# Attention, ELU layer and gated layer on one core: which slots are handed out first at a stage border, where weight conversion runs, and the order of VectorE's work beside the gated products

## The chip, the cores and the metric

The kernel runs on one core of a Trainium2 chip. The metric is the device time of one execution in microseconds (us); the profile's times are counted from the first instruction of the profiled execution. Engines are TensorE (PE), VectorE (DVE), ScalarE (ACT), GpSimd (POOL) and SyncE (SP). SP and POOL issue the transfers here, each from a queue of its own in program order.

## The reference

Chunked attention (chunks of 64) on q, k, v of shape 8 x 8 x 576 x 64, then two dense layers on the 4608 x 512 result:

```python
attn = softmax(q_c @ k_c.T / 8)              # per chunk of 64
x = (attn @ v_c).transpose(0, 2, 1, 3).reshape(4608, 512)
h = x @ w_in                                 # 512 -> 2048
x = where(h > 0, h, exp(min(h, 0)) - 1) @ w_out      # 2048 -> 512
out = (sigmoid(x @ w_gate) * (x @ w_val)) @ w_out2   # 512 -> 1536 -> 512
```

## The kernel before, in words

Every engine executes its instructions in the order in which the code emits them (a manual schedule); engines meet only through semaphores. There are four stages.

**Stage 1** (to about 511 us in the profile) walks nine blocks of 512 tokens. A block has eight slots, one for each 256 columns of the first layer. A slot `d` has the attention of one pair of tiles on PE and then 24 matmuls of the first layer (L380, `layer_in`) into one of three PSUM banks. The ELU of the slot before is taken by ACT (L394, L397) and VectorE (L402) into a tile of the pool `e`, which has four tiles, and stored by SP as `gd<-elu` (L405). The attention is done one block early, so in the last block only the layer and the ELU remain; that block is emitted by `stage_2` through `one`.

**Weight conversion.** The float64 weights of the later layers are converted on the chip in 26 pairs of tiles (`convert_pairs`). A pair has 12 steps in the list `todo`; `bg(n)` emits the next n of them between other work. A step is a few operations of ACT and VectorE; a pair loads two raw tiles (`craw`) and stores seven sums (`wd_glu<-ch` for the gate and value weights). A store is issued by POOL and waits for VectorE. Pairs 0 to 16 are spread over stage 1's slots, pairs 17 to 19 are begun in its last block, pairs 20 to 25 in stage 3.

**Weight fetches.** The 28 tiles of the pool `w` are shared by the 16 tiles of the first layer, the conversion's tiles and the fetched weights of the later stages. `hold(at, room, ahead)` emits, on POOL's queue, the fetches (L324) of the next `ahead` weight tiles that the products will use, never holding more than `room`; `room(7)` leaves 7 of the 28 tiles to the conversion. What does not fit is dropped and fetched again when its turn comes.

**Stage 2** (511 to 876 us) is the second layer. A round j (six of them, each for 768 tokens) has seven products i, each in four parts p; a part is 12 matmuls (L692) with one weight tile and one tile `gc`. The tile for part p of product i+1 is made beside part p of product i: a cast on ACT (L92) and a subtraction on VectorE (L98), of data that SP loads as `b<-gd` and VectorE has added up (L676). All these tiles are 6 KB slots per partition ("sixes"): ten on the right side and four on the left, where the first layer's inputs and the ELU tiles of stage 1 have lain. `get` takes the next slot from the list `idle`, `free` puts one back at its end. A left slot can be written only when the stores of the ELU tiles under it have read them.

**Stage 3** (876 to 1413 us) is gate and value: 36 units of seven products (banks x, w, y, z, x, y, z), each 12 matmuls (L828). Products 4 to 6 add onto banks of products 0 to 3, so product 5 (bank y) cannot start before VectorE has read bank y after product 2. VectorE adds the banks up (L101) and forms gate times value (L880, L882, `finish`). Six units share their inputs; in the sixth ("last") the next six's inputs are split (cast on ACT, L98 on VectorE) and in the fourth ("third" in the code, from the end) their sums are formed. **Stage 4** is the output layer (L960).

Names of the part that the change touches:

```python
PAIRS_1, PAIRS_2 = 17, HF + 2 * QU           # 17 and 20
need = list(soon)[:min(ahead, room)]         # in hold
p = idle.pop(0)                              # in get
```

Of the kernel before, what the change touches and what calls it, by code (L numbers as in the profile page):

```python
# [27 lines left out]
F1 = DFF1 // 128  # L28
# [6 lines left out]

LEAD = 11
EARLY = 2
PRE_STEPS = (0, 0, 1, 1, 1, 1, 1, 1, 1, 1, 2, 1)
W_AT = (1, 4)
IN_STEPS = 3  # L40
# [17 lines left out]
def kernel(  # L58
# [41 lines left out]
    def add(out, a, b):  # L100
        nc.vector.tensor_tensor(out=out, in0=a, in1=b, op=ALU.add)  # L101
# [3 lines left out]
    def bg(n):  # L105
        for _ in range(min(n, len(todo))):
            todo.pop(0)()
# [222 lines left out]
    def open_sixes(side, n):  # L330
        six[side] = ctx.enter_context(tc.tile_pool(name=f"six_{side}", bufs=n, side=side, reuse_waits="tile"))
        idle.extend([side] * n)

    def shaped(t, shape):
# [3 lines left out]
        names = " ".join("abc"[:len(shape)])  # L338
        return t[:, 0:n].rearrange(f"p ({names}) -> p {names}", **dict(zip("abc", shape)))

    def get(key, shape, dtype=F32):
        p = idle.pop(0)
        t = six[p].tile([128, 1536], dtype, tag="six", name=key)
        v = shaped(t, shape)
        owner[id(v)] = p, v
        return v
# [7 lines left out]
    def stage_1():  # L354
# [60 lines left out]
        with (  # L415
# [194 lines left out]
            convert_pairs(range(PAIRS_1), nc.gpsimd)  # L610
            end = (NB - 1) * HF
            for d in range(HF, end):
                slot(d, -(-len(todo) // (end - d)))
            assert not todo
        pb.close()
        return one
# [1 line left out]
    def room(*busy):  # L618
        return NW - sum(busy)
# [30 lines left out]
    def stage_2(one):  # L650
# [131 lines left out]

        open_sixes("right", 10)
        end = NB * HF
        convert_pairs(range(PAIRS_1, PAIRS_2), nc.gpsimd)
        for n in range(HF):
            one(end - HF + n, True)
            if n in (0, 2, 4):
                load_b(0, ("b11", "b12", "b22")[n // 2])
            if 2 <= n <= 5:  # L790
                split_b(0, 0, n - 2)
            if n >= 6:
                sub_b(0, "b11", "b12", "b11", n - 6)
            bg(3)
            hold(0, room(F1 - 2 * n - 2, 7), n + 2)
        for j in range(NJ):
            for i in range(7):
                for p in range(QM):
                    product(j, i, p)
                    if j == i == p == 0:  # L800
                        one(end, False)
                        pa.close()
                        open_sixes("left", 4)
                        three_p = ctx.enter_context(
                            tc.tile_pool(name="three", bufs=3, side="right", reuse_waits="tile")
                        )
                    beside(j, i, p)
                    if j == NJ - 1:
                        for f in first_x.get((i, p), ()):
                            f()  # L810
                    if i in (2, 3, 5) and p > 0:
                        bg(2)
                    hold((7 * j + i) * QM + p + 1, room(7 if todo else 0), 10)
                after(j, i)
        assert not todo and not raw and not gc

# [2 lines left out]
    def unit(n):  # L819
        j, q = seq[n]  # L820
        last, third = n % QU == QU - 1, n % QU == QU - 3
        for i, c in enumerate(PRODUCTS):
            ps = bank[c][:, :, 0:NL]
            w = held["glu", q, i]
            for b in range(2):
                for k in range(2):
                    for p, (zw, zx) in enumerate(PASSES):
                        nc.tensor.matmul(  # L828
                            out=ps[:, b],
                            lhsT=w[:, b, zw, 128 * k:128 * k + 128],  # L830
                            rhs=xc[j, i][:, zx, k],
                            start=(i < 4 and k == 0 and p == 0),
                            stop=(k == 1 and p == 2),
                            skip_group_check=True,
                        )
            if last:
                free(xc.pop((j, i)))
            yield
            hold(MID + 7 * n + i + 1, room(7 if todo else 0), 14 if n < len(seq) - 3 else 22)
            if i == 0:  # L840
                s, t = get("s", (2, 2, NL)), get("t", (2, 2, NL))
                u, v, c12 = s[:, 0], s[:, 1], t[:, 0]

                def sigmoid(x, of=None):
                    nc.scalar.activation(out=x, in_=x if of is None else of, func=ACTF.Sigmoid)  # L845

                nc.scalar.copy(out=u, in_=ps)  # L847
                while pending:
                    pending.pop(0)()
            elif i == 1:  # L850
                add(u, ps, u)
            elif i == 2:
                add(v, ps, u)
            elif i == 3:
                add(v, ps, v)
                sigmoid(v[:, 0])
            elif i == 4:
                sigmoid(t[:, 1, 0], ps[:, 0])
                nc.vector.tensor_tensor(out=t[:, 1, 0], in0=ps[:, 1], in1=t[:, 1, 0], op=ALU.mult)
            elif i == 5:  # L860
                add(c12, ps, u)
                sigmoid(c12[:, 0])
            else:
                add(u, ps, u)
                sigmoid(u[:, 0])
            bg(1)
            if j + 1 < NJ:
                if n % QU == 1 and i >= 5:
                    load_x(j + 1, i - 5)
                if third and 1 <= i <= 3:  # L870
                    sum_x(j + 1, i)
                if last:
                    if i == 6:
                        sum_x(j + 1, 4)
                    split_x(j + 1, i)
                    if i == 6:
                        done_x(j + 1)

        def finish():
            nc.vector.tensor_tensor(out=s[:, :, 0], in0=s[:, :, 1], in1=s[:, :, 0], op=ALU.mult)  # L880
            nc.sync.dma_start(out=gvd[j][:, 0:2, q], in_=s[:, :, 0])
            nc.vector.tensor_tensor(out=c12[:, 0], in0=c12[:, 1], in1=c12[:, 0], op=ALU.mult)  # L882
            nc.sync.dma_start(out=gvd[j][:, 2:4, q], in_=t[:, :, 0])
            free(s)
            free(t)
        pending.append(finish)

    def stages_3_4():
# [82 lines left out]
        def after(g, i):  # L971
# [28 lines left out]
                del ut[g], ot[g]  # L1000

        N = len(seq)
        before = {
            (N - 2, 1): lambda: load_g(0, "c12"),
            (N - 2, 2): lambda: load_g(0, "c22"),
            (N - 1, 1): lambda: load_g(0, "c11"),
            (N - 1, 2): lambda: sum_1(0),
            (N - 1, 3): lambda: load_g(0, "c21"),
            (N - 1, 5): lambda: (split_g(0, 0, "c11", keep=True), sum_2(0)),
        }  # L1010
        for n in range(N):
            if n == 2:
                hold(MID + 7 * n, room(7), 14)
                convert_pairs(range(PAIRS_2, len(tiles_of)), nc.sync)
            for i, _ in enumerate(unit(n)):
                before.get((n, i), lambda: None)()
        for g in range(G):
            for i in range(7):
                prepare(g, i)
# [68 lines left out]
```

## Time and profile before

| | |
|---|---|
| median of 3 runs | 1690.31 us (1690.2 to 1693.1) |
| the profiled execution's own time | 1689.72 us |
| its span, first to last instruction | 1688.0 us |
| PE busy | 1632.2 us, 97% of the span |
| VectorE, ACT, POOL busy | 1214.1, 744.6, 224.0 us |
| mean granted TensorE clock | 0.991 |
| transferred | 367.83 MB, 218 GB/s over the span |

The profiled execution takes 1.72 us more than its span and is 0.59 us under the median. PE is busy nearly throughout, so a saving can only come from the stretches in which it stands still or runs on a lower clock; those must be looked for stretch by stretch.

### The profile page before, as it was taken

What the parts mean: (1) busy time and instruction counts of PE and PEld (TensorE: products, weight loads), DVE (VectorE), ACT (ScalarE), POOL (GpSimd) and SP (SyncE); (2) the same over time, 40 slices, a digit from 0 to 9 for tenths busy, and PEclk for the clock granted to TensorE, in tenths of its full rate; (3) what the DMA queues carried; (4) which work ended last, traced back from release to release, by engine and by line L of the source; (5) the groups of instructions that cost most, each with busy time, mean ns of one, the idle gap of its engine ahead of it and who ended that gap; (6) DMA issues with size and microseconds to landing.
All of it is one profiled execution on the core that took longest, in us unless ns stands there. A gap on an engine that the chain in (4) does not pass through costs nothing.

```text
span 1688.0 us, 28556 instructions
## 1 busy us (share of the span) xinstructions
PE 1632.2 (97%) x11484; PEld 1527.7 (91%) x11484; DVE 1214.1 (72%) x1660; ACT 744.6 (44%) x1184; POOL 224.0 (13%) x368
## 2 busy tenths in 40 slices
PE   5899999999997999999999999999999999999998
PEld 4667777777786999999999999999999999999998
DVE  6878888887765877777776877656565646777776
ACT  4766767666663444444442433322131313333333
POOL 3322111211022100000121121201010120000000
PEclk9999999999998999999999999999999999999999
DMA  6558888888599943352897689757263598464541
GB/s 222 193 189 293 296 295 280 284 276 264 195 366 391 330 143 128 113 178 96 250 285 249 208 301 316 255 187 236 83 212 113 181 302 245 123 167 119 164 137 51
DMA packets 225972, 367.83 MB, mean 218 GB/s; under 512 B 13744, under 2 KB 133552, under 8 KB 224816
## 3 DMA queue, kind: packets, MB, share of 16 engines
q1 hardware_dynamic: 169344, 203.46, 37.2%
q0 software_dynamic: 56496, 162.55, 29.2%
q8 instruction: 90, 1.47, 0.4%
q14 instruction: 42, 0.34, 0.1%
HBM read 233.31 MB, written 132.64 MB: 217 GB/s over the span
## 4 chain that ended last, share of the span: by engine, by line
PE 77%; DVE 8%; DMA 6%; ACT 4%; issue 3%; POOL 1%; SPq 1%; ACTq 0%; DVEq 0%; POOLq 0%
PE bank_x L828 7%; PE bank_y L828 7%; PE bank_z L828 7%; PE bank_y L692 6%; PE bank_z L692 6%; PE bank_y L380 6%; PE bank_x L692 5%; PE bank_w L380 5%; PE bank_z L380 5%; PE bank_y L960 5%; PE bank_z L960 5%; PE bank_x L960 4%; PE bank_w L828 3%; PE bank_w L692 3%; DMA w<-wd_glu 2%
## 5 line engine op out<-in xcount | busy, mean ns | idle before, releaser
L98 DVE TENSOR_TENSOR gc<-b,gc 128x768 fp32r<-128x768 f32 x144 | 134.1, 954 | 61.8 <-ACT gc L92 60.5
L92 ACT CAST gc<-b 128x768 fp32r<-128x768 f32 x144 | 117.2, 834 | 129.3 <-PE bank_y L692 46.1
L828 PE MATMUL bank_y<-xc,w 128*128 128x384 f32 x864 | 163.7, 338 | 8.1 <-DVE s L101 7.5
L828 PE MATMUL bank_x<-xc,w 128*128 128x384 f32 x864 | 161.7, 336 | 0.5 <-ACT s L847 0.5
L828 PE MATMUL bank_z<-xc,w 128*128 128x384 f32 x864 | 161.9, 336 | 0.0
L828 PEld LDWEIGHTS bank_y<-xc,w 128*128 128x128 f32 x864 | 152.1, 189 | 9.7 <-DVE s L101 8.7
L828 PEld LDWEIGHTS bank_x<-xc,w 128*128 128x128 f32 x864 | 150.7, 188 | 1.1 <-ACT s L847 0.8
L828 PEld LDWEIGHTS bank_z<-xc,w 128*128 128x128 f32 x864 | 151.4, 188 | 0.0
L845 ACT ACTIVATE s<-s 128x384 f32<-128x384 f32 x72 | 37.8, 526 | 255.1 <-DVE s L101 255.1
L380 PE MATMUL bank_y<-xs,w 128*128 128x512 f32 x576 | 141.5, 401 | 4.8 <-ACT w L92 3.1
L324 POOL DMA_DIRECT2D w<-wd_glu x126 | 67.3, 537 | 583.9 <-PE bank_x L692 257.1
L380 PE MATMUL bank_w<-xs,w 128*128 128x512 f32 x576 | 139.8, 398 | 0.9 <-POOL w L98 0.9
L380 PE MATMUL bank_z<-xs,w 128*128 128x512 f32 x576 | 139.0, 397 | 0.0
L380 PEld LDWEIGHTS bank_y<-xs,w 128*128 128x128 f32 x576 | 108.8, 192 | 28.4 <-ACT w L92 3.5
L380 PEld LDWEIGHTS bank_w<-xs,w 128*128 128x128 f32 x576 | 107.1, 189 | 23.4 <-POOL w L98 1.2
L380 PEld LDWEIGHTS bank_z<-xs,w 128*128 128x128 f32 x576 | 107.8, 190 | 22.4
L101 DVE TENSOR_TENSOR s<-bank_z,s 128x768 f32<-128x768 f32 x72 | 68.8, 956 | 47.7 <-PE bank_z L828 47.1
L692 PE MATMUL bank_y<-gc,w 128*128 128x384 f32 x576 | 102.2, 336 | 0.0
L692 PE MATMUL bank_x<-gc,w 128*128 128x384 f32 x576 | 102.0, 336 | 0.0
L692 PE MATMUL bank_z<-gc,w 128*128 128x384 f32 x576 | 102.0, 336 | 0.0
L692 PEld LDWEIGHTS bank_y<-gc,w 128*128 128x128 f32 x576 | 100.4, 188 | 0.0
L692 PEld LDWEIGHTS bank_x<-gc,w 128*128 128x128 f32 x576 | 100.2, 188 | 0.1
(144 smaller groups left out, 2961.2 us busy)
## 6 DMA issues: line engine op xcount, KB each, us to landing
w<-wd_glu POOLq DMA_DIRECT2D x126, 512.0 KB, 6.7
gd<-elu SPq DMA_DIRECT2D x72, 512.0 KB, 3.6
c<-gv SPq DMA_DIRECT2D x72, 384.0 KB, 4.9
wd_glu<-ch POOLq DMA_DIRECT2D x36, 512.0 KB, 5.3
b<-gd SPq DMA_DIRECT2D x24, 768.0 KB, 7.1
w<-wd_mid POOLq DMA_DIRECT2D x32, 512.0 KB, 13.4
raw<-in_qkv SPq DMA_DIRECT2D x61, 256.0 KB, 3.9
gv<-s SPq DMA_DIRECT2D x36, 384.0 KB, 5.0
```

The lines of the kernel that those rows point to most:

```text
L92: nc.scalar.copy(out=out, in_=raw)
L98: lo_eng.tensor_sub(out=lo, in0=raw, in1=hi)
L101: nc.vector.tensor_tensor(out=out, in0=a, in1=b, op=ALU.add)
L324: nc.gpsimd.dma_start(out=t, in_=wd[m][q][:, (RIGHT if m == "out2" else LEFT)[i]])
L380: nc.tensor.matmul(out=h_bank(d)[:, n], lhsT=w[:, zw, kk * 128:(kk + 1) * 128], rhs=xs[j, kk][:, zx], start=(kk == 0 and p == 0), stop=(kk ...
L692: nc.tensor.matmul(out=bank[PRODUCTS[i]][:, u, 0:NL], lhsT=w[:, k, zw, 128 * u:128 * u + 128], rhs=t[:, zx, k], start=(i < 4 and p == 0 an ...
L828: nc.tensor.matmul(out=ps[:, b], lhsT=w[:, b, zw, 128 * k:128 * k + 128], rhs=xc[j, i][:, zx, k], start=(i < 4 and k == 0 and p == 0), sto ...
L845: nc.scalar.activation(out=x, in_=x if of is None else of, func=ACTF.Sigmoid)
L960: nc.tensor.matmul(out=po[c][:, m], lhsT=t[:, zx, q % 3, 128 * m:128 * m + 128], rhs=w[:, q % 2, zw], start=(i < 4 and q == 0 and p == 0 a ...
```

## The change

Five things are done.

1. **Slots.** While the first product of the first round of stage 2 runs (`right_first` is filled), `get` takes a right slot if one is idle, and a left one otherwise. Afterwards the order is that of the list again.
2. **Conversion in stage 1.** Pairs 0 to 16 are finished four slots earlier; in those last four slots of block 7 one weight tile more is held ahead in each. In block 8, where 2 to 9 tiles were held ahead and at most 7 + 2n, 5 to 12 are held ahead.
3. **Pairs 17 to 19** are not begun in block 8 any more, but at the start of round 1 of stage 2, and their steps run in rounds 1 and 2; 8 tiles instead of 7 are left to them.
4. **Gate and value.** The conversion's steps pause in each last and third unit, and 9 tiles instead of 7 are left to it. `finish` of a unit moves behind the addition of the next unit's product 1, `sum_x(.., 4)` moves from product 6 to 5, and the loads and sums for stage 4 (`beside`) are emitted behind a product's evacuation and earlier by one to two units for the loads.
5. Line numbers move by up to 9.

```diff
+SLACK = 4
 ...
+    right_first = []
     def get(key, shape, dtype=F32):
-        p = idle.pop(0)
+        p = idle.pop(idle.index("right") if right_first and "right" in idle else 0)
...
             for d in range(HF, end):
-                slot(d, -(-len(todo) // (end - d)))
+                slot(d, -(-len(todo) // max(end - SLACK - d, 1)))
+                if d >= end - SLACK:
+                    hold(0, room(F1), d - end + SLACK + 1)
...
-        convert_pairs(range(PAIRS_1, PAIRS_2), nc.gpsimd)
         for n in range(HF):
             one(end - HF + n, True)
...
-            bg(3)
-            hold(0, room(F1 - 2 * n - 2, 7), n + 2)
+            hold(0, room(F1 - 2 * n - 2), SLACK + 1 + n)
...
                     if j == i == p == 0:
                         one(end, False)
                         pa.close()
+                        right_first.append(True)
                         open_sixes("left", 4)
...
-                    if i in (2, 3, 5) and p > 0:
+                    if (j, i, p) == (1, 0, 0):
+                        hold(7 * QM, room(8), 10)
+                        convert_pairs(range(PAIRS_1, PAIRS_2), nc.gpsimd)
+                    if i in (2, 3, 5) and p > 0 and j > 0:
                         bg(2)
-                    hold((7 * j + i) * QM + p + 1, room(7 if todo else 0), 10)
+                    hold((7 * j + i) * QM + p + 1, room(8 if todo else 0), 10)
+                right_first.clear()
                 after(j, i)
...
-            yield
-            hold(MID + 7 * n + i + 1, room(7 if todo else 0), 14 if n < len(seq) - 3 else 22)
+            hold(MID + 7 * n + i + 1, room(9 if todo else 0), 14 if n < len(seq) - 3 else 22)
...
                 nc.scalar.copy(out=u, in_=ps)
+            elif i == 1:
+                add(u, ps, u)
                 while pending:
                     pending.pop(0)()
-            elif i == 1:
-                add(u, ps, u)
...
-            bg(1)
+            if not last and not third:
+                bg(1)
...
                 if last:
-                    if i == 6:
+                    if i == 5:
                         sum_x(j + 1, 4)
                     split_x(j + 1, i)
...
+            yield
...
-        before = {
-            (N - 2, 1): lambda: load_g(0, "c12"),
-            (N - 2, 2): lambda: load_g(0, "c22"),
-            (N - 1, 1): lambda: load_g(0, "c11"),
+        beside = {
+            (N - 4, 0): lambda: load_g(0, "c12"),
+            (N - 3, 0): lambda: load_g(0, "c22"),
+            (N - 2, 0): lambda: load_g(0, "c11"),
             (N - 1, 2): lambda: sum_1(0),
-            (N - 1, 3): lambda: load_g(0, "c21"),
-            (N - 1, 5): lambda: (split_g(0, 0, "c11", keep=True), sum_2(0)),
+            (N - 1, 3): lambda: (load_g(0, "c21"), sum_2(0)),
+            (N - 1, 5): lambda: split_g(0, 0, "c11", keep=True),
```

PE's instructions and their order are the same. What moves on the other engines is shown at three places.

ACT at the border from stage 1 to stage 2, before: the last ELU, the four casts for product 1 of round 0 (`gc`), the copy of product 0. What stands in brackets are the semaphores that the instruction waits for; `DMAHW0` to `DMAHW7` are those that SP's transfers use in turn, and the last ELU store of stage 1 has `DMAHW1`, the fourth last `DMAHW6`.

```order
L394 ACTIVATE elu<-bank_z 128x1024 [waits DMAHW1_49,PE_49]
L397 ACTIVATE elu<-elu 128x1024 [waits Activation_49]
L92 CAST gc<-t_5745 128x768 [waits DVE_49]
L92 CAST gc<-t_5745 128x768 [waits DMAHW6_49,DMAHW1_49]
L92 CAST gc<-t_5783 128x768 [waits DVE_49]
L92 CAST gc<-t_5783 128x768 [waits PE_49]
```

The same place in the changed kernel:

```order
L397 ACTIVATE elu<-bank_z 128x1024 [waits DMAHW1_49,DVE_49,PE_49]
L400 ACTIVATE elu<-elu 128x1024 [waits Activation_49]
L93 CAST gc<-t_5675 128x768 [waits DVE_49]
L93 CAST gc<-t_5675 128x768 [waits PE_49]
L93 CAST gc<-t_5707 128x768 [waits DMAHW6_49,DMAHW1_49,DVE_49]
L93 CAST gc<-t_5707 128x768 [waits PE_49]
```

The wait for the ELU stores has moved from the second cast (part 1) to the third (part 2); the second waits for PE alone.

POOL's queue from the last pair of stage 1 on, before (`craw` are raw tiles to convert, `wd_glu<-ch` converted sums to store, `w<-wd_mid` weight fetches for stage 2):

```order
L277 DMA wd_glu_86<-ch 128x2x512 x2
L196 DMA craw<-in_w_val 128x1024 x2
L324 DMA w<-wd_mid_78 128x1024
L324 DMA w<-wd_mid_79 128x1024
L196 DMA craw<-in_w_gate 128x1024 x2
L324 DMA w<-wd_mid_80 128x1024
L277 DMA wd_glu_86<-ch 128x2x512
L324 DMA w<-wd_mid_81 128x1024
L277 DMA wd_glu_86<-ch 128x512
L277 DMA wd_glu_86<-ch 128x2x512 x2
```

In the changed kernel all 28 fetches of round 0 follow that pair, and the first raw tile comes behind them:

```order
L278 DMA wd_glu_86<-ch 128x2x512 x2
L325 DMA w<-wd_mid_78 128x1024
L325 DMA w<-wd_mid_79 128x1024
L325 DMA w<-wd_mid_80 128x1024
L325 DMA w<-wd_mid_81 128x1024
...
L197 DMA craw<-in_w_val 128x1024 x2
L325 DMA w<-wd_mid_78 128x1024
L197 DMA craw<-in_w_gate 128x1024 x2
L325 DMA w<-wd_mid_79 128x1024
```

Between a fetch and the next there is no store that waits for VectorE any more until round 1. Over the program POOL has 57 fetches of `wd_mid` instead of 32 and 139 of `wd_glu` instead of 126.

VectorE in the first last unit (unit 5) of gate and value, before (L101 adds a bank up, L98 splits the next inputs, L276, L217 and L221 are conversion):

```order
L98 TENSOR_TENSOR xc<-x,xc 128x768
L101 TENSOR_TENSOR s<-bank_w,s 128x768
L276 TENSOR_TENSOR ch<-cs,ch 128x2x256
L98 TENSOR_TENSOR xc<-x,xc 128x768
L101 TENSOR_TENSOR s<-bank_y,s 128x768
L276 TENSOR_TENSOR ch<-cs,ch 128x2x256
L98 TENSOR_TENSOR xc<-x,xc 128x768
L101 TENSOR_TENSOR s<-bank_z,s 128x768
L217 TENSOR_SCALAR ct<-ct 128x1024
```

The same unit in the changed kernel (L102 is the addition, L99 the split, L889 and L891 are `finish`):

```order
L99 TENSOR_TENSOR xc<-x,xc 128x768
L102 TENSOR_TENSOR s<-bank_w,s 128x768
L889 TENSOR_TENSOR s<-s 128x2x384
L891 TENSOR_TENSOR t<-t 128x384
L99 TENSOR_TENSOR xc<-x,xc 128x768
L102 TENSOR_TENSOR s<-bank_y,s 128x768
L99 TENSOR_TENSOR xc<-x,xc 128x768
L102 TENSOR_TENSOR s<-bank_z,s 128x768
L99 TENSOR_TENSOR xc<-x,xc 128x768
```

One conversion operation per product is gone from this unit, and `finish`, which stood ahead of the addition of bank w, now stands behind it.

## Rows read from the trace of the kernel before

**Rows 1.** The page: span, and busy time of TensorE.
```profile
span 1688.0 us, 28556 instructions
PE 1632.2 (97%) x11484; PEld 1527.7 (91%) x11484; DVE 1214.1 (72%) x1660; ACT 744.6 (44%) x1184; POOL 224.0 (13%) x368
```
**Rows 2.** Windows: length, busy us of each engine, granted clock, DMA share, GB/s.
```profile
0.00:50.00 50.00, 30.50 (x436) 21.98 (x440) 31.53 (x63) 25.18 (x52) 18.29 (x35) 0.97 0.57 196
50.00:130.00 80.00, 70.12 (x611) 54.55 (x601) 65.80 (x108) 53.36 (x89) 20.82 (x20) 0.96 0.63 210
...
500.00:540.00 40.00, 27.76 (x130) 25.03 (x129) 19.87 (x23) 13.29 (x17) 11.19 (x20) 0.83 1.12 388
540.00:880.00 340.00, 340.00 (x1958) 340.00 (x1957) 262.38 (x259) 146.59 (x187) 22.31 (x41) 1.00 0.60 196
```
**Rows 3.** Timeline of TensorE at the border: start, duration, instructions, idle before.
```profile
511.02 8.48 PE L692 MATMUL bank_x<-gc,w 128*128 128x384 f32 x48
...
533.85 9.14 PE L692 MATMUL bank_w<-gc,w 128*128 128x384 f32 x36 [12.24 <-ACT gc L92]
542.84 8.53 PE L692 MATMUL bank_y<-gc,w 128*128 128x384 f32 x48
551.20 8.48 PE L692 MATMUL bank_z<-gc,w 128*128 128x384 f32 x48
```
**Rows 4.** Timeline of ACT at the border.
```profile
532.97 0.83 ACT L92 CAST gc<-t 128x768 fp32r<-128x768 f32 x1 [15.84 <-DMA gd<-elu]
```
**Rows 5.** The chain that ended last, its piece at the border: start, length.
```profile
514.63 18.32 DMA gd<-elu
```
**Rows 6.** Transfers from 460 to 545 us: totals, and issues with median us to landing.
```profile
DMA packets 16034, 31.60 MB, mean 372 GB/s; under 512 B 975, under 2 KB 7110, under 8 KB 16031
...
w<-wd_mid POOLq DMA_DIRECT2D x23, 512.0 KB, 13.5
gd<-elu SPq DMA_DIRECT2D x11, 512.0 KB, 9.4
```
**Rows 7.** The ELU stores' line over the whole run: us from issue to landing.
```profile
DMA to landing us min/median/max: 3.0/3.6/19.1
```
**Rows 8.** Timeline of TensorE in gate and value and into stage 4.
```profile
949.54 2.24 PE L828 MATMUL bank_x<-xc,w 128*128 128x384 f32 x12
...
1054.04 3.75 PE L828 MATMUL bank_y<-xc,w 128*128 128x384 f32 x12 [2.04 <-DVE s L101]
...
1076.70 2.24 PE L828 MATMUL bank_x<-xc,w 128*128 128x384 f32 x12
...
1397.46 2.24 PE L828 MATMUL bank_x<-xc,w 128*128 128x384 f32 x12
...
1423.59 4.44 PE L960 MATMUL bank_y<-w,gc 128*128 128x256 f32 x36
1427.87 2.40 PE L960 MATMUL bank_z<-w,gc 128*128 128x256 f32 x19
```
**Rows 9.** Window of round 2 of stage 2; columns as in rows 2.
```profile
628.00:686.50 58.50, 58.50 (x339) 58.50 (x338) 43.43 (x41) 24.06 (x30) 0.00 (x0) 1.00 0.40 136
```
**Rows 10.** VectorE by line and form: count, busy us, mean ns, idle before.
```profile
L98 DVE TENSOR_TENSOR xc<-x,xc 128x768 fp32r<-128x768 f32 x42 | 40.1, 955 | 19.6 <-ACT xc L92 19.5
L859 DVE TENSOR_TENSOR t<-bank_x,t 128x384 f32<-128x384 f32 x36 | 20.0, 556 | 39.9 <-ACT t L845 39.9
L221 DVE TENSOR_SCALAR ct<-ct 128x1024 uint32<-128x1024 uint32 x26 | 17.9, 690 | 0.5
L276 DVE TENSOR_TENSOR ch<-ct,ch 128x256 fp32r<-128x256 f32 x26 | 10.9, 418 | 0.0
```
**Rows 11.** Timelines of VectorE and TensorE in unit 18, behind a last unit without conversion.
```profile
1157.16 0.96 DVE L101 TENSOR_TENSOR s<-bank_y,s 128x768 f32<-128x768 f32 x1
...
1160.02 2.24 PE L828 MATMUL bank_y<-xc,w 128*128 128x384 f32 x12
```
**Rows 12.** Timeline of POOL in block 8.
```profile
489.55 0.72 POOL L277 DMA_DIRECT2D wd_glu<-ch  x1 [18.24 <-DVE ch L276]
```

More of the change, by code (lines that the diff above doesn't have):

```diff
@@ L1012, in stages_3_4 @@
             if n == 2:
-                hold(MID + 7 * n, room(7), 14)
+                hold(MID + 7 * n, room(9), 14)
                 convert_pairs(range(PAIRS_2, len(tiles_of)), nc.sync)
             for i, _ in enumerate(unit(n)):
-                before.get((n, i), lambda: None)()
+                beside.get((n, i), lambda: None)()
         for g in range(G):
```

## The prediction

> **What bounds the kernel now.** The page's totals come first: TensorE is busy 1632.2 of 1688.0 us [rows 1], so 55.8 us of standing still is all that any edit of the other engines can win, apart from matmuls on the lower clock. The windows say where these lie [rows 2]. The first 130 us lose 19.50 and 9.88 us; the change moves nothing there (the first step it moves stands in slot 44 of 72). From 500 to 540 us 12.24 us are missing, and the granted clock is 0.83. From 540 to 880 us, all of stage 2 behind the border, nothing is missing: 340.00 of 340.00. What is left lies in gate and value and at its end.
>
> *The border.* In TensorE's timeline [rows 3] product 0 of round 0 starts at 511.02 and product 2 at 542.84. A product of 48 matmuls takes 8.36 us (542.84 to 551.20), so two should have taken 16.72; they took 31.82. So 15.10 us are lost: 12.24 in one wait in front of part 1 of product 1, and 2.7 because the 36 matmuls behind it took 8.99 us where 36/48 of 8.36 are 6.27. The wait is for a cast on ACT, and that waited 15.84 us for the store of an ELU tile [rows 4]. The chain shows the store: issued at 514.63, it lands 18.32 us later [rows 5]. Such a store lands after 3.6 us in the median of the run, 3.0 at the least [rows 7]; around the border the median of eleven is 9.4, with 31.60 MB moved in 85 us, at 372 GB/s [rows 6]. So two things make the wait: a slot that needs the last store is wanted early, and the store is slow because the transfers are saturated.
>
> *Gate and value.* Unit 13 starts at 1076.70 and unit 35 at 1397.46: 22 units in 320.76 us, 14.58 each, undisturbed. Units 5 to 12 (949.54 to 1076.70) took 127.16 where eight take 116.64: 10.52 us lost, in waits like that at 1054.04 for VectorE's addition, and in slower matmuls behind them. From 1397.46 to the third product of stage 4 (1423.59) it took 26.13, where a unit and two products of 4.28 (1423.59 to 1427.87) are 23.14: 2.99 lost [rows 8]. In reach are thus 15.10 + 10.52 + 2.99 = 28.6 us.
>
> **The change, part by part.**
>
> *Slots at the border.* The part that needs the last store becomes part 2 of product 1 instead of part 1; the other casts wait for TensorE or VectorE only, as the order shows. The store itself is issued when it was, about 514.63, since the ELU in front of it hangs on TensorE alone. Part 2 is due when product 0 and two parts of 2.09 us (8.36 / 4) are through: 511.02 + 8.36 + 4.18 = 523.56. The cast takes 0.83 [rows 4], and VectorE's subtraction 0.95, of which the first two passes need nothing; so the store must land by about 521.7 to cost nothing, which leaves it 7.1 us. With the shift alone and the store as slow as before, the wait shrinks by 2.09 us only, so the rest must come from the next part.
>
> *Conversion out of block 8, fetches brought forward.* For three pairs, six raw tiles of 0.5 MB and 21 sums of 0.25 MB leave the stretch: 3.1 + 5.5 = 8.7 MB, less the part that lay outside. The weight fetches stay the same 28 x 0.5 MB, but POOL, with no store that waits for VectorE between them, may issue them as tiles of the first layer come free, two in a slot of 5.5 us, and be nearly through when the last store is issued. From 467 to 514 us I count about 16 fetches (8 MB, less the last ones), nine ELU stores (4.7 MB) and three loads of `b` (4.7 MB): 17 MB in 47 us, 360 GB/s against 372 granted [rows 6]. Most of the three loads lies before 505 us, so the last two slots ask for less than is granted, and the queue should be short at 514.63. I take a landing between 3.6 us [rows 7] and 7.1, hence no wait at all and no slower matmuls behind it: 15.1 us gained. The bounds: 9.4 us, the median under saturation [rows 6], leaves 2.3 us of waiting; 18.32 leaves 11.2 and the slow matmuls.
>
> Against the second half of this stands the Trainium skill, page "DMA: Bandwidth & Descriptors", section "Issuing engines are not separate DMA queues": transfers of all issuing engines run on the same 16 DMA engines and interleave. By that, fetches issued earlier on POOL's queue take their bandwidth from the ELU stores and loads on SP's, and if POOL pours out all fetches it may, the store could stay at the saturated latency; the sum would then be 2.3 us worse.
>
> *Conversion in stage 1, four slots earlier.* 204 steps over 52 slots instead of 56 are 4 in a slot almost throughout, where before 4 fell to 3 after 36 slots. TensorE loses nothing while 4 steps run in each slot, so I cost it at nothing; the cover is VectorE's free time there.
>
> *Pairs 17 to 19 in rounds 1 and 2.* A pair has nine VectorE operations of some 0.69 us and five of 0.42 [rows 10]: 8.3 us, so 1.5 pairs in a round are 12.4. Round 2 of before has VectorE busy 43.43 of 58.5 us [rows 9]; with that it is 55.9, still under 58.5. A slot is free again when its product's part is done and due three parts (6.3 us) later; cast and subtraction take 1.8 of that, so a lag of up to some 4.5 us is hidden. Products 2, 3 and 5 carry 6 steps each, about 4.1 us on top of four subtractions and an addition (4.8): 8.9 against 8.36, a lag of 0.5 us each. Nothing lost; if the cover goes, the next product waits by what exceeds 4.5. The 25 additional fetches (13 MB) and the 8.7 MB of the pairs in two rounds of 58.5 us are 185 GB/s on top of 136 [rows 9], together 321, below what was granted at the border. Cost nothing; bound 0 to 33 us (second rival).
>
> *Gate and value.* A unit has five additions of 0.96, `finish` of 0.96 + 0.56, and a product of 0.56 (the 0.56 by the half-wide row): 6.9 us. A last unit adds seven splits and one sum of 0.955: 14.5 of 14.58, no room. Before, seven conversion steps lay on top (7/12 of 8.3, 4.8 us) in units 5 and 11: 19.3 us of work in 14.58. That is the lag which ends in the waits. In units 17, 23 and 29 of before there are no steps, and no wait: in unit 18 the addition of bank y ends at 1158.12, and the product that overwrites it starts at 1160.02, 1.9 us later [rows 11]. The changed units 5 and 11 are like these. Two steps of the next unit (1.4 us) now stand ahead of that addition in units 6, 12 and 18, but the sum moved to product 5 spares ACT's wait for it, about 0.9; margin 1.4. So I take 10.0 of the 10.52, keeping 0.5 for these three places. The 13 more fetches of `wd_glu` (6.7 MB over 16 units, 29 GB/s) I cost at nothing.
>
> *Into stage 4.* `sum_2` runs two products earlier and the additions no longer stand behind it. What stays is the first split: behind the addition of c12 (0.96), a sigmoid (0.5) and the cast (0.83) it comes 2.3 us after product 5, when product 6 takes 2.08; with the low part about 0.7 us. So 2.3 of 2.99 gained; bounds 0 and 2.99.
>
> **Sum.** 15.1 + 10.0 + 2.3 = 27.4 us, from the profiled execution's own time: 1689.72 - 27.4 = 1662.3. That execution lies 0.6 us under the median of the runs, so I say 1663.
>
> **The rivals.**
> 1. *The store stays late.* For it: all fetches may now press into the same 45 us, and the store still stands in the way of part 2. Against: 8.7 MB gone, and the loads done before. It gives 1663 + 2.3 = 1665 at 9.4 us, up to 1663 + 11.2 + 2 = 1676 at 18.3. In the last case the change did not do there what it says.
> 2. *Weights late in rounds 1 and 2: slower than before.* POOL issues in order, and fetches now stand behind conversion stores that wait for VectorE. POOL has waited 18.24 us at such a store [rows 12]; with 13.5 us to land [rows 6] a fetch behind it comes after 31.7 us, where ten parts ahead are 20.9: TensorE would wait 10.8 us. Three pairs have six such groups of stores. From the third late group on (32 us) the gain is eaten; four give 1663 + 43 = 1706. Against: the long wait came with nothing due (no weight was waited for in rows 3), since POOL was ahead of VectorE; and from 540 to 880 us, with the twelve steps of a pair left in round 0, TensorE lost nothing [rows 2]. One late group would give 1674.
> 3. *Gate and value keeps its waits,* at other places: conversion now reaches unit 18, in 19 instead of 21 tiles. Three starts of units with a wait of 2.04, as in rows 8, and slow matmuls behind it (3.75 - 2.24 = 1.5): 10.6 us, 1673.
>
> **How the numbers follow.** Forecast 62%; first rival 18% (1665 to 1676); third 8%; one or two late groups 8% (1674 to 1685); second rival in full 3%; 1% for an answer below all that I count. A measurement of this kernel tells about 0.2%, 3.4 us, from no change. Faster by more is everything but the full second rival and a part of its neighbours: 0.95; same 0.02; slower 0.03. The floor is 1689.72 - 28.6 = 1661.1, and the runs vary by some 1 us below that; the range reaches from 1660 to 1676, which leaves out some 1 in 10. The likeliest case alone is 1661 to 1666.
>
> **What would show it.** Border: product 2 of round 0 starts at about 527.8, 16.7 us after product 0, no idle time in front of part 2 or less than 2.3 us, and the last ELU store lands in under 7.1 us. Rounds 1 and 2: TensorE without idle time, VectorE busy near 56 of 58.5 us. Gate and value: units 5 to 12 take 116.6 to 117.2 us. Wrong would be a wait for `w<-wd_mid` in rounds 1 and 2, a wait for VectorE in units 6, 12 or 18, or a store that lands later than 7.1 us.

## The result

| | before | after |
|---|---|---|
| median | 1690.26 us (1689.78 to 1693.1, 4 runs) | 1666.78 us (1666.08 to 1668.19, 4 runs) |
| profiled execution, its span | 1689.72, 1688.0 us | 1666.74, 1664.7 us |

The ratio is 0.9859, 95% interval 0.9842 to 0.9876: the change makes the kernel 1.4% faster. The forecast was 1663 us; the time lies 3.8 us above it and 0.8 us outside the likeliest case's own range (1661 to 1666), inside the range of 1660 to 1676.

### The profile page after: what moved, and what is told of

It reads as the page before. It is cut to its first block, busy times and chain, and to the rows that moved or that the text cites. A ratio compares the mean times of both kernels' runs of the same rounds, so it can differ in the third digit from the quotient of the medians.

```text
span 1664.7 us, 28666 instructions
## 1 busy us (share of the span) xinstructions
PE 1624.6 (98%) x11484; PEld 1522.4 (91%) x11484; DVE 1207.9 (73%) x1660; ACT 742.5 (45%) x1184; POOL 244.4 (15%) x406
## 4 chain that ended last, share of the span: by engine, by line
PE 79%; DVE 10%; ACT 5%; DMA 2%; issue 2%; POOL 0%; SPq 0%; ACTq 0%; DVEq 0%; POOLq 0%
PE bank_y L836 8%; PE bank_z L836 8%; PE bank_x L836 8%; PE bank_y L697 6%; PE bank_z L697 6%; PE bank_x L697 6%; PE bank_z L969 5%; PE bank_y L969 5%; PE bank_x L969 5%; PE bank_y L383 4%; PE bank_w L836 4%; PE bank_w L383 4%; PE bank_z L383 4%; PE bank_w L697 3%; PE bank_w L969 2%
## 5 line engine op out<-in xcount | busy, mean ns | idle before, releaser
L99 DVE TENSOR_TENSOR gc<-b,gc 128x768 fp32r<-128x768 f32 x144 | 134.2, 954 | 45.8 <-ACT gc L93 45.6
L325 POOL DMA_DIRECT2D w<-wd_glu x139 | 74.4, 538 | 398.4 <-PE bank_x L836 135.3
L697 PEld LDWEIGHTS bank_z<-gc,w 128*128 128x128 f32 x576 | 100.3, 188 | 0.0
```

What stands on the lines that cost most here:

```text
L99: lo_eng.tensor_sub(out=lo, in0=raw, in1=hi)
L325: nc.gpsimd.dma_start(out=t, in_=wd[m][q][:, (RIGHT if m == "out2" else LEFT)[i]])
L697: nc.tensor.matmul(out=bank[PRODUCTS[i]][:, u, 0:NL], lhsT=w[:, k, zw, 128 * u:128 * u + 128], rhs=t[:, zx, k], start=(i < 4 and p == 0 an ...
```

## The profile after

The page: span and busy time of TensorE, to compare with [rows 1].

```profile
span 1664.7 us, 28666 instructions
PE 1624.6 (98%) x11484; PEld 1522.4 (91%) x11484; DVE 1207.9 (73%) x1660; ACT 742.5 (45%) x1184; POOL 244.4 (15%) x406
```

The windows, columns as in [rows 2]; the last row is round 2 of stage 2, as in [rows 9].

```profile
500.00:540.00 40.00, 40.00 (x218) 38.17 (x217) 27.24 (x24) 17.14 (x21) 2.65 (x5) 1.00 0.81 281
540.00:880.00 340.00, 340.00 (x1958) 340.00 (x1957) 269.11 (x281) 152.53 (x200) 44.16 (x80) 1.00 0.73 238
...
627.30:685.70 58.40, 58.40 (x338) 58.40 (x337) 54.16 (x65) 29.82 (x42) 11.41 (x20) 1.00 0.92 307
```

The border lost 12.24 us in [rows 2] and loses nothing now, at the full clock. Round 2 now has the conversion beside it: VectorE busy 54.16 of 58.40 us (forecast 55.9), 307 GB/s (forecast 321), TensorE without a gap.

TensorE's timeline at the border, and ACT's cast for part 2 of product 1; they answer to [rows 3] and [rows 4].

```profile
510.50 8.48 PE L697 MATMUL bank_x<-gc,w 128*128 128x384 f32 x48
518.82 8.52 PE L697 MATMUL bank_w<-gc,w 128*128 128x384 f32 x48
527.17 8.53 PE L697 MATMUL bank_y<-gc,w 128*128 128x384 f32 x48
...
520.62 1.57 ACT L93 CAST gc<-t 128x768 fp32r<-128x768 f32 x2 [3.29 <-DVE t L681]
```

From product 0 to product 2 it takes 527.17 - 510.50 = 16.67 us instead of 31.82. The view puts the cast's wait down to VectorE's sum:

```profile
518.38 1.75 DVE L681 TENSOR_TENSOR t<-b,b 128x1536 f32<-128x1536 f32 x1
```

But this sum is through at 518.38 + 1.75 = 520.13, and the last ELU store, issued at 514.1, lands after 6.5 us, at 520.6. The cast starts then, at 520.62: it still waits for the store. (In `finish_back` below the sum is through at 518.37, the store lands at 519.1, and the cast starts at 519.19.) What has changed is that nothing is lost by it, since part 2 is due only at 510.50 + 8.36 + 4.18 = 523.04.

TensorE in gate and value: the product on bank w in units 0 and 35, all waits between them, and the start of stage 4; to compare with [rows 8].

```profile
863.00 2.27 PE L836 MATMUL bank_w<-xc,w 128*128 128x384 f32 x12
...
901.62 2.35 PE L836 MATMUL bank_y<-xc,w 128*128 128x384 f32 x12 [0.86 <-DVE s L102]
...
960.89 2.37 PE L836 MATMUL bank_y<-xc,w 128*128 128x384 f32 x12 [0.57 <-DVE s L102]
...
1094.15 2.36 PE L836 MATMUL bank_y<-xc,w 128*128 128x384 f32 x12 [1.49 <-DVE s L102]
...
1378.02 2.27 PE L836 MATMUL bank_w<-xc,w 128*128 128x384 f32 x12
...
1390.95 0.74 PE L969 MATMUL bank_x<-w,gc 128*128 128x256 f32 x4 [0.25 <-ACT gc L93]
1391.94 3.91 PE L969 MATMUL bank_x<-w,gc 128*128 128x256 f32 x32 [0.26 <-DVE gc L99]
...
1399.97 4.40 PE L969 MATMUL bank_y<-w,gc 128*128 128x256 f32 x36
```

Three waits are left, in units 2, 6 and 15, all in front of bank y. In before the same two rows of bank w are:

```profile
878.62 2.24 PE L828 MATMUL bank_w<-xc,w 128*128 128x384 f32 x12
...
1399.54 2.24 PE L828 MATMUL bank_w<-xc,w 128*128 128x384 f32 x12
```

So the span's 23.3 us split by four marks:

| from, to | before | after | gained | forecast |
|---|---|---|---|---|
| start, unit 0 | 878.62 | 863.00 | 15.62 | 15.1 |
| unit 0, unit 35 | 520.92 | 515.02 | 5.90 | 10.0 |
| unit 35, third product of stage 4 | 24.05 | 21.95 | 2.10 | 2.3 |
| from there to the end | 264.41 | 264.73 | -0.32 | 0 |

Of the first 15.62 the border gave 31.82 - 16.67 = 15.15; the other 0.5 lies in stage 1, whose end falls between 508.06 and 512.16 us in the twelve executions profiled, so it says nothing. What has to be explained is the second line.

## The experiments

Three groups, each on one chip with its own runs of the kernel before (1691.57, 1691.16 and 1689.47 us in the median). Theories for the missing 4.1 us: the *finish* theory, that `finish`, moved behind the addition of bank w, now delays the addition of bank y; the *pause* theory, that the conversion steps cost what they did and the pause only moved them (third rival); the *chance* theory, that it belongs to the execution and not to the kernel. For the border the question is which carries it, the slots (part 1) or the transfers (parts 2 and 3, which no run parts fully).

**control**: the changed kernel again.

> The changed kernel itself once more, for the spread. In its profile a unit without a wait takes 14.61 us, in that of the kernel before 14.58, about 1 us over 36 units. If that belongs to the kernel, it is there again (14.60 to 14.62); if it belongs to an execution, it is not. The time: 1666.8 within 1 us.

1665.55 us, ratio 0.9853 (0.9836 to 0.9869). The three waits stand at the same places (0.37, 0.57, 1.53 us) and a unit without a wait takes 14.60 to 14.62 us again, not the 14.58 of before. The chance theory falls, but for some 0.5 us in unit 2, whose interval from bank w to bank w is 15.72 us in the changed kernel, 15.24 here and 15.05 in `fetch_late` and `lead_5` below.

**finish_back**: `finish` back in front of the addition.

```diff
-            elif i == 1:
-                add(u, ps, u)
                 while pending:
                     pending.pop(0)()
+            elif i == 1:
+                add(u, ps, u)
```

> The changed kernel with finish back in product 0 of the next unit. In the changed kernel TensorE waits for VectorE in units 2 (0.86 us), 6 (0.57) and 15 (1.49). Theory A: two of them come from finish standing behind the addition of product 1: in unit 2 it is caught behind the first conversion step, which waits for raw tiles, and in unit 15 the sum of the next inputs takes a slot whose store finish has only just issued. Then units 2 and 15 lose their waits, unit 6 keeps its 0.57 since VectorE works without a pause there and finish stands ahead of the addition of bank y either way: 2.4 us and the slow matmuls behind, 2.7 to 3.3 us less than the changed kernel, about 1663.8. Theory B: the waits come from the longer stretch of conversion and the raw tiles' transfers alone; then all three stay, 1666.8 within 1 us.

1662.81 us, ratio 0.9834 (0.9819 to 0.9849), 2.7 us less than the control on the same chip. Units 2 and 6 no longer wait at all, unit 15 waits 0.40. That unit 6 lost its wait too was not expected; the part on gate and value below says why. VectorE in unit 2, first of the changed kernel:

```profile
897.15 0.75 DVE L218 TENSOR_SCALAR ct<-ct 128x1024 f32<-128x1024 f32 x1 [5.84 <-ACT ct L206]
897.82 0.94 DVE L102 TENSOR_TENSOR s<-bank_w,s 128x768 f32<-128x768 f32 x1
898.68 0.94 DVE L889 TENSOR_TENSOR s<-s 128x768 f32<-128x768 f32 x1
899.54 0.55 DVE L891 TENSOR_TENSOR t<-t 128x384 f32<-128x384 f32 x1
900.01 0.68 DVE L222 TENSOR_SCALAR ct<-ct 128x1024 uint32<-128x1024 uint32 x1
900.62 0.94 DVE L102 TENSOR_TENSOR s<-bank_y,s 128x768 f32<-128x768 f32 x1
```

and the same unit with `finish` in front (from the run `finish_back_2` below):

```profile
893.56 0.96 DVE L889 TENSOR_TENSOR s<-s 128x768 f32<-128x768 f32 x1 [0.59 <-ACT s L852]
894.44 0.55 DVE L891 TENSOR_TENSOR t<-t 128x384 f32<-128x384 f32 x1
896.06 0.69 DVE L218 TENSOR_SCALAR ct<-ct 128x1024 f32<-128x1024 f32 x1 [1.07 <-ACT ct L206]
896.67 0.95 DVE L102 TENSOR_TENSOR s<-bank_w,s 128x768 f32<-128x768 f32 x1
...
898.28 0.96 DVE L102 TENSOR_TENSOR s<-bank_y,s 128x768 f32<-128x768 f32 x1
```

Both start with a conversion step that waits for ACT. In the first, `finish` and a step lie between the additions of banks w and y; VectorE has stood idle for 5.84 us just before, with `finish` queued behind the wait. In the second, `finish` is done inside that idle time.

**no_pause**: the steps run in every unit again.

```diff
-            if not last and not third:
-                bg(1)
+            bg(1)
```

> The changed kernel with a conversion step in every product of every unit from unit 2 on, as before, so with no pause in last and third units. Theory A: the pause is what took away the waits of units 5, 6, 11 and 12; seven steps of 0.69 us on top of 14.5 in a unit of 14.58 bring them back: 4 to 7 us more than the changed kernel, 1671 to 1674, with waits for VectorE or ACT behind units 5 and 11. Theory B: the two more tiles for the conversion did it, since ACT no longer stands in front of a store; then no difference, 1666.8 within 1 us.

1670.78 us, ratio 0.9881 (0.9866 to 0.9896), 5.2 more than the control. Six waits instead of three, the longest 2.21 and 1.89 us, in units 12 and 6. So the pause does heal, and the pause theory falls.

**glu_alone**: the kernel before with part 4 of the change alone.

> The kernel before with only the edits in gate and value and into stage 4; border, slots and stages 1 and 2 as before. If the parts add up: 1690.3 less 5.9 (gate and value) less 2.1 (into stage 4), so 1682 to 1683, with the 12.2 us wait at the border as before. If the gains hang together (the waits in gate and value depend on how the border went), it lies outside 1680 to 1685.

1680.2 us, ratio 0.9935 (0.992 to 0.995), inside the bounds of 1680 to 1685 but 1.8 us under the 1682 expected, although the border waits 14.45 us here. Unit 0 to unit 35 takes 513.51 us, 7.4 less than before; a unit without a wait takes 14.58. Waits of 0.45, 0.60 and 0.99 us are left, in units 2, 6 and 12. So unit 15's wait is not of part 4 alone, and the longer units are not of part 4 at all.

**slots_alone**: the kernel before with part 1 alone (`right_first` and its use in `get`).

> The kernel before with only the new order of slots at the border. Theory A: the part that needs the last ELU store comes one part later, the store itself stays as slow (18.3 us), so the wait of 12.2 us shrinks by 2.1: 1688.2, within 1687 to 1689.5. Theory B: the order of slots is the cure and the store was only slow because of what stood behind the wait; then the wait is under 4 us and the time 1676 to 1680.

1689.16 us, ratio 0.9995 (0.9984 to 1.0005): no difference that can be measured. TensorE's wait and ACT's cast at the border:

```profile
531.97 6.41 PE L694 MATMUL bank_w<-gc,w 128*128 128x384 f32 x24 [10.60 <-ACT gc L92]
...
531.08 1.56 ACT L92 CAST gc<-t 128x768 fp32r<-128x768 f32 x2 [15.54 <-DMA gd<-elu]
```

The last store lands after 18.7 us, and the wait shrinks from 12.24 to 10.60 only.

**no_slots**: the changed kernel without part 1.

```diff
-        p = idle.pop(idle.index("right") if right_first and "right" in idle else 0)
+        p = idle.pop(0)
```

> The changed kernel with slots taken from the head of the list again. Theory A: the pause of the conversion has already brought the last ELU store down to 6.5 us (issued at 514.1, landed at 520.6); part 1 is due at 520.9 and its cast takes 0.83, so TensorE waits 0.3 to 1 us: 1667 to 1668, hardly to be told from the changed kernel. Theory B: the order of slots carries the border's gain; then a wait of several us with slow matmuls behind it is back, 1672 to 1682.

1667.38 us, ratio 0.9873 (0.9857 to 0.9889). TensorE at the border, and ACT's second cast:

```profile
509.98 8.48 PE L697 MATMUL bank_x<-gc,w 128*128 128x384 f32 x48
...
521.25 0.62 PE L697 MATMUL bank_w<-gc,w 128*128 128x384 f32 x2 [0.68 <-ACT gc L93]
...
529.71 8.53 PE L697 MATMUL bank_y<-gc,w 128*128 128x384 f32 x48
...
520.37 0.83 ACT L93 CAST gc<-t 128x768 fp32r<-128x768 f32 x1 [4.28 <-DMA gd<-elu]
```

Part 1 waits for the store again, and three shorter waits follow, one of 0.52 us for a cast and two of 0.38 us for VectorE's subtraction. Product 0 to product 2 takes 19.73 us. Without the slots 31.82 - 19.73 = 12.1 us of the border's 15.15 are won by the transfers; the slots add 3.06. Units take 14.58 us here.

**fetch_late**: the changed kernel with the fetches written later (none in block 7, `n + 2` ahead in block 8).

```diff
-                if d >= end - SLACK:
-                    hold(0, room(F1), d - end + SLACK + 1)
...
-            hold(0, room(F1 - 2 * n - 2), SLACK + 1 + n)
+            hold(0, room(F1 - 2 * n - 2), n + 2)
```

> The changed kernel without the four fetches in block 7, and with the smaller number held ahead in block 8 (2 to 9, as before). Theory A: POOL's queue holds the same 28 fetches in a row either way, and POOL runs ahead as far as tiles are free, so the position in the code changes nothing: 1666.8 within 1 us, last store at 6 to 7 us. Theory B: fetching earlier is what cleared the queue for the last ELU stores; then the store is later than 7.1 us and TensorE waits at the border, 1668 to 1676.

1666.44 us, ratio 0.9862 (0.9846 to 0.9879): as the changed kernel. POOL issues a fetch every 2.72 us, each when TensorE lets go of a tile, in both kernels; the last leaves 3 us before the last ELU store in both. Once no store of the conversion stands on the queue, where the fetch is written does not matter. So of part 2 the earlier fetches are not what heals the border; that leaves part 3 and the conversion's earlier end.

**lead_5**: weight tiles held 5 parts ahead instead of 10 in rounds 1 and 2, to price the second rival.

```diff
-                    hold((7 * j + i) * QM + p + 1, room(8 if todo else 0), 10)
+                    hold((7 * j + i) * QM + p + 1, room(8 if todo else 0), 5 if todo else 10)
```

> The changed kernel, but while the pairs 17 to 19 are converted (rounds 1 and 2 of stage 2) weight tiles are held five parts ahead instead of ten, a lead of 10.4 us instead of 20.9. Theory A, the prediction's second rival: a wait of POOL at a store delays the fetch behind it by the length of that wait; the changed kernel's POOL waited 26.57, 19.11 and 16.06 us there, so with some 5 us to land a fetch comes 31, 24 and 21 us after its turn, against 10.4 us of lead: TensorE waits for w<-wd_mid by 10 to 20 us per such group, and the kernel is 20 to 60 us slower than the changed one, 1687 to 1727. Theory B: POOL stands at the store because it has run ahead of the other engines; the store is issued when VectorE comes to its place in the program, and a fetch behind it leaves with its five parts of lead nearly whole. Then TensorE loses nothing between 569 and 686 us, or at most some 2 us, and the time is that of the changed kernel, 1665 to 1669.

1680.32 us, ratio 0.9942 (0.9925 to 0.9958), some 15 us more than the changed kernel (0.9859 of 1689.47 is 1665.6): neither theory. All waits of TensorE in rounds 1 and 2:

```profile
618.14 10.35 PE L697 MATMUL bank_y<-gc,w 128*128 128x384 f32 x48 [5.74 <-DMA w<-wd_mid]
...
672.43 3.49 PE L697 MATMUL bank_z<-gc,w 128*128 128x384 f32 x12 [4.33 <-DMA w<-wd_mid]
677.06 8.58 PE L697 MATMUL bank_x<-gc,w 128*128 128x384 f32 x48 [1.14 <-DMA w<-wd_mid]
```

In the chain, the fetch that ends the first of these waits; and in POOL's timeline the first store ahead of it:

```profile
608.87 9.14 DMA w<-wd_mid
...
605.24 1.27 POOL L278 DMA_DIRECT2D wd_glu<-ch  x2 [39.97 <-DVE ch L277]
```

POOL waited 39.97 us, but the fetch came at 608.87. It is for a product due at 603.90 + 8.34 = 612.24, so with a lead of five parts of 2.09 us its turn was at 601.8: it is 7.1 us late, not 40. POOL had run ahead, so most of its wait is no delay. The rest is: 7.1 + 9.14 us to land are 5.8 more than the lead of 10.4. The waits sum to 11.2 us, and matmuls on a clock of 0.94 and 0.97 in the two rounds add 3.7 (twelve products from 570.54 to 685.48 take 114.9 us where twelve of 8.34 are 100.1). Both theories were wrong in size; ten parts (20.9 us) would cover a lateness like this one, 16.2 us with the landing, with 4.7 us to spare.

**finish_no_slots** and **finish_back_2**: finish_back without part 1, and finish_back again beside it.

> The changed kernel with finish back in product 0 (as finish_back) and without the preference for right slots (as no_slots). If the waits of units 2 and 6 come from the place of finish alone, they are gone here too, and the sum of next inputs in unit 15 or 12 waits under 1 us. If the longer units (14.60 to 14.62 instead of 14.58 us) belong to the preference for right slots, they are 14.58 here, some 0.7 to 1 us less over 36 units. Against it stand the four short waits at the border, 2.0 us. The sum is finish_back plus 1 us, 1662 to 1666; if the units stay at 14.60 or more, the length of a unit does not hang on the order of slots.

> The kernel with finish back in product 0, once more, on the chip of the two others, so that the order of slots can be read from two kernels that differ in nothing else: 1661 to 1665, units of 14.60 to 14.62 us, one wait of some 0.4 us in unit 15, and no wait at the border.

1662.97 us, ratio 0.9844 (0.9829 to 0.9859), and 1662.44 us, ratio 0.9841 (0.9826 to 0.9855): the same within what can be measured. The parts differ: without part 1 the border takes 19.26 us instead of 16.68, 2.6 more, but unit 0 to unit 35 takes 510.42 instead of 511.64, 1.2 less: no wait at all, and 14.58 us a unit. In unit 15, for instance, the product on bank y takes 2.08 us to the next one without part 1 (1084.03 to 1086.11) and 2.10 with it (1085.86 to 1087.96).

## Why the prediction was right in the whole and wrong in one term

**Border, 15.1 us: right, 15.15.** Product 2 starts 16.67 us after product 0, as said (16.7). The store landed after 6.5 us, of the 7.1 allowed, and after 6.2 to 6.8 in all nine executions profiled with parts 2 and 3 of the change; it was 18.3, 18.7 and 20.5 in the three without them. Of the reason given, one half held: POOL's fetches are through when the last store is issued. The other half, that the last slots ask for less than is granted, did not: from 504 to 514 us 387 GB/s run in the changed kernel and 378 in before. So that the store kept inside 7.1 us was in part luck. The last four ELU stores from issue to landing, and what moved while the last one was under way, in all and on POOL's queue (`q0`: packets, MB), in before (514.63 to 532.95):

```profile
DMA to landing us min/median/max: 16.4/18.0/19.1
...
DMA packets 3111, 7.15 MB, mean 390 GB/s; under 512 B 223, under 2 KB 766, under 8 KB 3111
...
q0 software_dynamic: 1543, 4.42, 66.6%
```

and in the changed kernel (514.1 to 520.56):

```profile
DMA to landing us min/median/max: 6.5/11.3/12.7
...
DMA packets 1351, 2.59 MB, mean 401 GB/s; under 512 B 88, under 2 KB 656, under 8 KB 1351
...
q0 software_dynamic: 174, 0.58, 24.3%
```

The rate is the same; what is gone is what POOL's queue moved beside the store: 0.58 of 2.59 MB (22%) instead of 4.42 of 7.15 (62%). POOL in the kernel before, around and behind the last store, and in the changed kernel its last issue ahead of it:

```profile
511.69 1.95 POOL L277 DMA_DIRECT2D wd_glu<-ch  x3 [2.68 <-issue]
513.63 1.63 POOL L324 DMA_DIRECT2D w<-wd_mid  x3
515.72 0.53 POOL L324 DMA_DIRECT2D w<-wd_mid  x1 [0.46 <-PE bank_x L692]
...
531.96 0.53 POOL L324 DMA_DIRECT2D w<-wd_mid  x1 [1.08 <-DMA w<-wd_mid]
```

```profile
511.17 0.53 POOL L325 DMA_DIRECT2D w<-wd_mid  x1 [2.19 <-issue]
```

Held up by stores that waited for VectorE (8.69 us for the one at 507.75), POOL of before let three sums and four fetches go within 5 us around the last ELU store, and eight more fetches, one every 1.5 to 3 us, before that store landed. The changed kernel's POOL has sent its last fetch 3 us before the store. That these late transfers are the cause is read from the rows and from no_slots and slots_alone, which part the slots from the transfers; whether the bunch of seven or the fetches behind it weigh more was not tried. The rule of the Trainium skill weighed in the prediction ("DMA: Bandwidth & Descriptors", section "Issuing engines are not separate DMA queues") is that transfers of all issuing engines run on the same 16 DMA engines and interleave. The trace agrees: SP's store landed after 18.3 us with POOL's 4.42 MB beside it and after 6.5 with 0.58. The dearer outcome that the prediction drew from it, 2.3 us worse, did not come, since the fetches were through.

**Rounds 1 and 2, nothing: right.** No wait, VectorE and transfers near the forecast. The second rival's mechanism exists (lead_5), at 5.7 us for a late group with half the lead instead of 10.8 with the whole: it had taken POOL's wait for the delay of the fetch.

**Gate and value, 10.0 us: mis-sized, 5.9.** Two steps failed. The first is "margin 1.4", for units 6, 12 and 18. It was worked out from unit 18 of before, with `finish` in front of the addition of bank w, and for that order it is right: in `finish_back` the addition of bank y in unit 18 ends at 1131.79 and the product that overwrites it starts at 1133.17, 1.38 us later. In the changed kernel the same two are 0.35 us apart:

```profile
1136.76 0.95 DVE L102 TENSOR_TENSOR s<-bank_y,s 128x768 f32<-128x768 f32 x1
...
1138.06 2.27 PE L836 MATMUL bank_y<-xc,w 128*128 128x384 f32 x12
```

The count left out that `finish`, 0.94 + 0.55 us, now stands behind the addition of bank w, though it had the new order before it. The delay begins in the last unit. VectorE at the first split of unit 5, in the changed kernel and in `finish_back_2`:

```profile
940.04 0.96 DVE L99 TENSOR_TENSOR xc<-x,xc 128x768 fp32r<-128x768 f32 x1 [1.93 <-ACT xc L93]
```

```profile
940.60 0.96 DVE L99 TENSOR_TENSOR xc<-x,xc 128x768 fp32r<-128x768 f32 x1 [0.56 <-ACT xc L93]
```

Both splits start 2.84 us after the unit's product on bank w (937.20 and 937.76). In the second kernel `finish` is done before, while VectorE would stand idle for ACT; in the changed kernel it comes behind, and the unit's last split is 18.41 us from bank w instead of 17.06. With 14.5 of 14.58 us taken, the unit has no room to catch up, and unit 6 waits. At units 6, 12 and 18 this cost 0.84, 0.07 and 0 us. Units 5 to 12 together take 117.7 us, where 116.6 to 117.2 were forecast.

The second step that failed, and the larger in us, is to count these three places alone. Unit 2 takes 15.72 us from bank w to bank w instead of 14.62; there a conversion step holds VectorE up, and `finish` is caught behind it. Unit 15 has 16.37 instead of 14.60. There VectorE's sum of next inputs waits for the store that `finish` has just issued:

```profile
1088.23 0.55 DVE L891 TENSOR_TENSOR t<-t 128x384 f32<-128x384 f32 x1
1092.27 0.96 DVE L637 TENSOR_TENSOR x<-x 128x768 f32<-128x768 f32 x1 [3.48 <-DMA gv<-t]
```

The addition of bank y stands right behind this sum, whose slot is that of the product being stored. With `finish` earlier TensorE's wait is 0.40 us or less, and with other slots (no_slots, glu_alone, finish_no_slots) it is not there. In no_slots and glu_alone another place has the same trouble: in unit 11 ACT's cast of the next inputs waits 4.68 and 4.65 us for the store `gv<-s` that `finish` has issued; in no_slots the unit's last split then comes 18.82 us after bank w, against 17.36 in the changed kernel, and unit 12 waits 0.99 us; with `finish` earlier (finish_no_slots) the cast waits 1.45 and TensorE not at all. Last, the longer units: 35 of 14.60 to 14.62 us instead of 14.58 to 14.60 are 0.8 us. 1.1 + 0.9 + 1.8 + 0.8 = 4.6 for unit 2, for units 6 and 12, for unit 15 and for the longer units; less the 0.5 kept for units 6, 12 and 18 these are the 4.1 missing. The third rival had the number of waits right, three; but each costs 0.8 to 1.8 us and not 3.5, since no slow matmuls follow (2.36 us against 3.75 in [rows 8]; the granted clock is 1.00 from 1093 to 1099 us, and 0.72 from 1053 to 1059 in before). That finish_no_slots has all 10.5 us (520.92 - 510.42) shows that they were in reach.

**Into stage 4, 2.3 us: 2.10.** The split waits 0.25 + 0.26 us, near the 0.7 that the prediction kept.

**What stays open:** whether part 3 alone heals the border, and why the order of slots at the border, 350 us earlier, sets the length of a product.

**The faster version.** Both kernels with `finish` in product 0 beat the changed kernel by some 3 us, with 1662.4 to 1663.0 us.

## What to carry to other kernels

An operation moved out of one wait's way stands in another's. Here `finish` left a place where VectorE stood idle for one in a unit without room, and all that followed came 1.3 us later. So count, for each buffer that is overwritten, what now lies between the instruction that fills VectorE's queue and the one that frees the buffer, in the units where the queue starts late and not in a quiet one. A queue that issues in order and waits for another engine does not only delay its own transfers: what it held back is under way later, here beside a store of another queue, which landed after 18.3 us instead of 6.5. How long such a queue waits says how far it has run ahead, not how late the transfer behind it is; that is read from the transfer's due time. And where a wait is put down to an engine that was done before, look for what else the instruction waits for.

## What the hardware showed that was not expected

The same 12 matmuls of 128x384 take 2.08 or 2.10 us in two kernels that differ in nothing but the order in which slots are handed out. A unit without a wait takes 14.58 us (14.60 in the first six) in the four executions without the preference for right slots (before, glu_alone, no_slots, finish_no_slots) and 14.60 to 14.62 in all eight executions with it. And a 512 KB store landed after 6.5 us in the changed kernel and after 18.3 in before, with 401 and 390 GB/s running while it was under way: the rate alone does not tell how long one transfer takes.
